# Attention with beacon keys, then a SwiGLU layer, on one core: a new order in the first third of the instruction lists, and the last two projection pairs woven half by half

## The chip, the core and the metric

One core of a Trainium2 chip runs the whole program. The metric is the time of one execution on the device, in microseconds (us), and less is better. A kernel is timed in several executions; the median counts. One more execution is recorded by the hardware profiler, and all rows in this document come from such recordings. Instructions run on five engines, each with its own list in program order: TensorE (PE, with its weight loads shown as PEld), VectorE (DVE), ScalarE (ACT), GpSimd (POOL) and SyncE (SP). They wait for each other through semaphores.

## What is computed

```
scores = scale * np.matmul(q, k_all.transpose(0, 1, 3, 2))   # k_all = [beacon_k, k], 16 + 576 keys
scores = np.where(causal, -1000000000.0, scores)             # beacons are seen by all queries
a = np.exp(scores - scores.max(-1, keepdims=True))
a /= a.sum(-1, keepdims=True) + 1e-09
attn_out = np.matmul(a, v_all)                               # 8 batches, 8 heads, 576 rows, 64 wide
x = attn_out.transpose(0, 2, 1, 3).reshape(B * S, H * D)     # 4608 tokens, 512 wide
g = x @ w_gate                                               # 512 -> 1536
silu = g * (1.0 / (1.0 + np.exp(-g)))
out = (silu * (x @ w_val)) @ w_out                           # 1536 -> 512
```

Inputs and output are float32; the kernel multiplies in bfloat16.

## The kernel before, in words

The 4608 tokens are cut into 9 chunks of 512, the attention into 8 batches of 4 head pairs. All work is cut into small pieces, and one string of letters, `plan` (line 806), says in which order the pieces are written; each letter calls `piece` (line 732), which issues that piece's instructions on whatever engines it needs. So the string sets the order on every engine at once. No scheduler moves anything afterwards. The letters that matter here, each counted from 0 in its own kind:

- `l`: one load on POOL's DMA queue, from the list `order_of_loads` (line 720). From load 24 on (`FREE_LOADS`, line 53) POOL first waits until PE has passed an earlier piece.
- `g`/`f`: pair up q and k of a head pair, on DVE or POOL (the tile `side`). `T`: turn them on PE into a PSUM tile, `t_ps`. `Q`/`q` and `K`/`k`: copy the q half and the k half out of that tile into `qT` and `kT`; the capital letter puts the copy on DVE, the small one on ACT. The two halves lie in two banks of one tile.
- `S`/`s`: the score matmuls of one unit, a quarter of a head pair (`s_ps`). `E`: exp on ACT (`p`). `D`/`M`: the causal mask on DVE or POOL. `P`/`p`: the two halves of the product with v (`pv_ps`). `R`: normalise on DVE (`rec`, then `x`). `X` and `Y`/`y`: turn x of batch 0 on PE, copy it out on DVE or ACT.
- `G`/`H`: the two halves of a gate tile; each is 8 matmuls on 64 of the 128 array rows, which run two at a time (`gv_ps`). `a`: tanh on ACT (`th`). `1`, `2`: two steps on DVE, which write `u` and `hT`.
- `F`: a step of the output projection (`o_ps`), again matmuls on 64 rows in twos. 24 steps make a pair of 128-token tiles. The last of the 18 pairs is cut by columns at 384 into two parts. `O`/`o`: copy a tile out on DVE or ACT and store it.
- `h`: a keep-warm pair, two small matmuls that PE runs ahead of the next score or product piece, into that piece's own PSUM tile (`keep_warm`, line 176).

All PSUM tiles come from four slots of two banks, which `take` and `give` (lines 132 and 140) hand round first in, first out, in the order of the plan. A piece that takes a slot waits until the copy that reads the slot's last tile is done. In `halves` (line 154) the first half of a gate or projection writes one bank with the upper array rows and the other with the lower; the second half swaps them. Before the swap an empty PE instruction waits for the last matmul into the slot:

```
            last = max((w for (i, _), w in writers.items() if i == at[0]), key=lambda w: w[2])
            if was[3]:
                after(nc.tensor.nop(), last[1], "one bank, two row halves")
```

Of the kernel before, what the change touches and what calls it, by code (L numbers as in the profile page):

```python
# [52 lines left out]
FREE_LOADS = 24  # L53
# [33 lines left out]
def kernel(  # L87
# [66 lines left out]
    def halves(key, bank, row, o, l, r, start, stop, turn=False):  # L154
# [3 lines left out]
        if was is not None and was[0] != row:  # L158
            last = max((w for (i, _), w in writers.items() if i == at[0]), key=lambda w: w[2])
            if was[3]:  # L160
                after(nc.tensor.nop(), last[1], "one bank, two row halves")
            for other, w in writers.items():
                if other[0] == at[0]:
                    writers[other] = (w[0], w[1], w[2], False)
# [433 lines left out]
    CUT = 384  # L598

    def project(n):  # L600
        pr, s = divmod(n, 2 * NF)
        j, i = divmod(2 * pr, TOK // P)
        last = pr == NCH * 2 - 1
        parts = [(0, slice(0, DM), s)]
        if last:

            parts = [(0, slice(0, CUT), 2 * s), (0, slice(0, CUT), 2 * s + 1)] if s < NF else [
                (1, slice(CUT, DM), 2 * (s - NF)), (1, slice(CUT, DM), 2 * (s - NF) + 1)]
        for part, cols, st in parts:
            if st == 0:  # L610
                for bank in range(2):
                    key = ("f", pr, part, bank * last)
                    if key not in held:
                        ps = take(key, [P, 2, DM], FP32, "o_ps")
                    projected[pr, part, bank] = key, ps
            second, f = divmod(st, NF)
            for row in (1, 0) if second else (0, 1):
                bank = row ^ second
                key, ps = projected[pr, part, bank]
                k64 = slice(HALF * row, HALF * row + HALF)  # L620
                halves(
                    key, bank, row, ps[:, bank, cols],
                    hTs[j][k64, f, P * (i + bank) : P * (i + bank) + P], wo[k64, f, cols],
                    st == 0, st == 2 * NF - 1,
# [4 lines left out]
    def evacuate(n, eng):  # L629

        pr, bank = divmod(n, 2)
        part, cols = 0, slice(0, DM)
        if pr >= NCH * 2 - 1:
            part, cols = pr - (NCH * 2 - 1), (slice(0, CUT), slice(CUT, DM))[pr - (NCH * 2 - 1)]
            pr = NCH * 2 - 1
# [4 lines left out]
        key, ps = projected[pr, part, bank]  # L640
        copy(eng, o_sb[:, cols], ps[:, bank, cols])
        if bank == 1 or key[-1] != projected[pr, part, 1][0][-1]:
            give(key)
# [88 lines left out]
    def piece(kind):  # L732
        as_kind = {"s": "S", "M": "D", "k": "K", "q": "Q", "Y": "y", "o": "O", "i": "I", "A": "e", "f": "g"}.get(kind, kind)
# [78 lines left out]
    ll2ltGHal1G2lGHHa1aatlt21tGH1H2lattF2aGFH112FF2FFGSaEFlHt1GFFaHa2Gltl1t2GtlH12latH12Fa12FFGGtDHS
    ltlaE1FHFFaG2lSFHtl12allF12GFElMFllFHaSG1FEFHaGFFolMHl2l1G2aSOF1H2FaE1FtFG2sHFEaFslF1FDFlSE2FDFE
    DFSESlPpFFFRlDFFFlStFESSDFFEFFsEDFOPEpMPEOpSFFlFRMStRFEFEFSsFEMEFFDFFPplFSFFFFFlFRDSSEFEtFtSFDFF
    FFFEEFlVFFsoOElFFSFtFFDFtSMPEDEtSFElpSDRFFMFFtlMPtESSFEEpRFttFFGFDDSEGHFGa12HHlla1aG21FHl2aGlFHl
    1a2GSHD1ool2aDtPlEGM1ltp2HRlla1GtlSlGH2alEGHG1l2FaM1HHF2a1GFa2HS1FF2FSFFaEFSFEF12lFSPEFpDMFEFSlS
# [52 lines left out]
```

## Time and profile before

| | |
|---|---|
| median of 3 timed runs | 365.43 us (364.56 to 365.43) |
| span of the profiled execution, first to last instruction | 362.0 us |
| its own time outside the span | not listed; the span is 3.4 us below the median |
| PE busy | 352.9 us, 97% |
| DVE busy | 225.4 us, 62% |
| ACT busy | 187.6 us, 52% |
| POOL busy | 124.6 us, 34% |

A busy share is an average over stages, and a matmul's end in the records is modelled, so that a PE that is 97% busy need not do 97% of what it could. What PE really lost is found from the starts of neighbouring matmuls. In a timeline row, the brackets at the end give the idle time ahead of it and what ended that.

### The profile page before, as it was taken

How to read it: one execution, taken by the hardware profiler on the slowest of the kernel's cores; microseconds unless marked ns; L12 is line 12 of the kernel's file. 1: busy time of each engine (PE TensorE's matmuls, PEld its weight loads, DVE VectorE, ACT ScalarE, POOL GpSimd, SP SyncE). 2: the span in 40 equal slices, each digit the busy share in tenths (PEclk: the TensorE clock that was granted, in tenths of full speed). 3: DMA queues.
4: the chain of work that ended last, by engine and by line, in shares of the span. 5: the costliest groups of instructions: out<-in, count | busy, mean ns of one | idle time of the engine just before them, and what ended most of it. 6: DMA issues, size and time to landing. Idle time of an engine off the chain costs nothing.

```text
span 362.0 us, 11888 instructions
## 1 busy us (share of the span) xinstructions
PE 352.9 (97%) x5160; PEld 198.6 (55%) x5160; DVE 225.4 (62%) x439; ACT 187.6 (52%) x284; POOL 124.6 (34%) x188
## 2 busy tenths in 40 slices
PE   7799999999999999999999999999999999999996
PEld 3587565654444566554565566546655554455544
DVE  5577997566766654487528754776467764464342
ACT  4966999723434777544863576447633232221310
POOL 8945499926247545374423013111000000000000
PEclk9999999999999999999999999999999999999999
DMA  8999999999999999999979829502413000110113
GB/s 121 156 197 204 191 191 158 174 175 147 149 147 121 134 136 129 153 174 135 122 132 147 109 37 154 67 6 26 113 62 65 2 2 0 61 60 1 61 60 116
DMA packets 146132, 39.74 MB, mean 110 GB/s; under 512 B 131488, under 2 KB 141728, under 8 KB 146080
## 3 DMA queue, kind: packets, MB, share of 16 engines
q0 software_dynamic: 97424, 19.00, 72.1%
q1 hardware_dynamic: 48368, 19.79, 27.9%
q8 instruction: 40, 0.66, 0.8%
q10 hardware_dynamic: 288, 0.20, 0.2%
q14 instruction: 12, 0.10, 0.1%
HBM read 38.27 MB, written 9.44 MB: 132 GB/s over the span
## 4 chain that ended last, share of the span: by engine, by line
PE 85%; DMA 5%; POOL 5%; DVE 2%; ACT 1%; issue 1%; POOLq 0%
PE gv_ps L168 49%; PE o_ps L168 25%; DMA qk<-in_q_dram 5%; PE s_ps L168 5%; PE pv_ps L168 4%; PE pv_ps L493 2%; POOL qk L209 2%; POOL vb L219 1%; DVE x L522 1%; POOL wg L248 1%; POOL wv L248 1%; DVE p L414 1%; PE t_ps L166 0%; ACT p L405 0%; ACT th L579 0%
## 5 line engine op out<-in xcount | busy, mean ns | idle before, releaser
L168 PE MATMUL gv_ps<-xT,wv 64*128 64x512 bf16 (+2 forms) x912 | 203.2, 365 | 0.0
L168 PE MATMUL gv_ps<-xT,wg 64*128 64x512 bf16 (+2 forms) x912 | 202.8, 365 | 0.1
L579 ACT ACTIVATE th<-gv_ps 128x512 f32<-128x512 f32 (+2 forms) x114 | 65.4, 575 | 116.5 <-PE gv_ps L168 116.1
L405 ACT ACTIVATE p<-s_ps 128x832 bf16<-128x832 f32 (+2 forms) x127 | 104.3, 868 | 32.4 <-PE s_ps L168 28.7
L168 PE MATMUL o_ps<-wo,hT 64*128 64x512 bf16 (+2 forms) x912 | 116.5, 365 | 0.2
L584 DVE SCALAR_TENSOR_TENSOR u<-th,gv_ps 128x512 f32<-128x512 f32 (+2 forms) x114 | 74.7, 656 | 65.9 <-ACT th L579 65.1
L168 PEld LDWEIGHTS <-wg 64*128 64x128 bf16 x912 | 82.5, 94 | 45.9 <-PE gv_ps L168 2.4
L168 PEld LDWEIGHTS <-wv 64*128 64x128 bf16 x912 | 81.8, 94 | 40.1 <-issue 0.7
L591 DVE SCALAR_TENSOR_TENSOR hT<-gv_ps,u 128x512 bf16<-128x512 f32 (+2 forms) x114 | 74.7, 661 | 3.0
L168 PEld LDWEIGHTS <-hT 64*128 64x128 bf16 x912 | 42.3, 94 | 34.1 <-PE o_ps L168 1.2
L219 POOL DMA_DIRECT2D vb<-in_v_dram x40 | 33.9, 853 | 64.1 <-PE s_ps L168 25.7
L168 PE MATMUL s_ps<-qT,kT 64*128 64x336 bf16 (+3 forms) x512 | 43.0, 250 | 1.9 <-ACT kT L256 1.0
L168 PEld LDWEIGHTS <-kT 64*128 64x128 bf16 x512 | 23.8, 94 | 22.9 <-ACT kT L256 1.8
L219 POOL DMA_DIRECT2D qk<-in_q_dram x25 | 21.2, 851 | 25.7 <-PE gv_ps L168 7.1
L414 DVE TENSOR_TENSOR p<-p,upper 128x256 bf16<-128x256 bf16 (+2 forms) x84 | 24.0, 317 | 9.8 <-ACT p L405 8.1
L522 DVE TENSOR_TENSOR x<-pv_ps,rec 128x640 bf16<-128x640 f32 (+1 forms) x32 | 25.3, 791 | 1.2
L521 DVE RECIPROCAL rec<-pv_ps 128x10 f32<-128x10 f32 (+1 forms) x32 | 6.8, 213 | 28.1 <-PE pv_ps L168 22.7
L258 DVE COPY o_sb<-o_ps 128x512 f32<-128x512 f32 (+2 forms) x20 | 12.7, 654 | 17.0 <-PE o_ps L168 13.9
L219 POOL DMA_DIRECT2D qk<-in_k_dram x25 | 21.3, 856 | 5.4 <-PE gv_ps L168 4.3
L418 POOL TENSOR_SCALAR_AFFINE_SELECT p<-p 128x256 bf16<-128x256 bf16 (+2 forms) x46 | 17.4, 399 | 14.0 <-ACT p L405 13.8
L168 PEld LDWEIGHTS <-p 64*128 64x128 bf16 x960 | 18.8, 94 | 4.5 <-PE pv_ps L168 0.2
L168 PE MATMUL pv_ps<-vb,p 64*128 64x65 bf16 x960 | 19.9, 189 | 0.0
(65 smaller groups left out, 141.4 us busy)
## 6 DMA issues: line engine op xcount, KB each, us to landing
out_dram<-o_sb SPq DMA_DIRECT2D x34, 256.0 KB, 2.6
vb<-in_v_dram POOLq DMA_DIRECT2D x24, 128.0 KB, 5.7
qk<-in_q_dram POOLq DMA_DIRECT2D x21, 128.0 KB, 5.6
qk<-in_k_dram POOLq DMA_DIRECT2D x16, 128.0 KB, 5.9
wo<-in_moe_w_out_dram POOLq DMA_DIRECT2D x2, 768.0 KB, 10.1
wg<-in_moe_w_gate_dram POOLq DMA_DIRECT2D x3, 384.0 KB, 11.7
wv<-in_moe_w_val_dram POOLq DMA_DIRECT2D x3, 384.0 KB, 14.2
qk<-in_k_dram POOLq DMA_DIRECT2D x2, 576.0 KB, 11.5
```

The costliest lines, as they stand in the source:

```text
L168: ins = nc.tensor.matmul(o, lhsT=l, rhs=r, start=start, stop=stop)
L209: return nc.gpsimd.dma_start(qk[b % 2][base : base + HALF, RUN * h0 : RUN * h1] .rearrange("p (h e) -> p h e", e=RUN)[:, :, D * i0 : D * i ...
L219: return nc.gpsimd.dma_start(dst[p0 : p0 + n, c, :, 0:D], src[b, :, r : r + n, :].rearrange("h j d -> j h d"))
L248: nc.gpsimd.dma_start(t[:, :, cols], src[:, cols].rearrange("(kk p) f -> p kk f", p=P))
L258: eng.tensor_copy(o, i)
L405: nc.scalar.activation(p_of(b, m, u == "A")[:, :, c0 : c0 + w], ps[:, :, 0:w], ACT.Exp, scale=0.125)
L414: nc.vector.tensor_tensor(out=ap, in0=ap, in1=upper[:, None, d : d + w].to_broadcast([P, 2, w]), op=ALU.mult)
L418: nc.gpsimd.affine_select(out=ap, in_=ap, compare_op=ALU.is_ge, fill=0.0, base=d, pattern=[[0, 2], [1, w]], channel_multiplier=-1,)
L522: nc.vector.tensor_tensor(out=xs[b][:, c0:NKT, P * m : P * m + P].rearrange("p c (h d) -> p h c d", d=D), in0=o[:, :, :, 0:D], in1=rec[:, ...
L579: nc.scalar.activation(th[:, 0:w], gvs[n][:, 0, 0:w], ACT.Tanh, scale=0.5)
L584: nc.vector.scalar_tensor_tensor(out=u[:, 0:w], in0=ths[n][:, 0:w], scalar=1.0, in1=gvs[n][:, 0, 0:w], op0=ALU.add, op1=ALU.mult)
L591: nc.vector.scalar_tensor_tensor(out=hTs[j][:, f, c0:c1], in0=gvs.pop(n)[:, 1, 0 : c1 - c0], scalar=0.5, in1=ths.pop(n)[:, 0 : c1 - c0], o ...
```

## The change

The order of pieces is new from the first gate half (piece 101 of 1756) to piece 467, some way into the gates of the next chunk but one; the last letters are new too. In the new stretch, five of the eight turns that feed batches 1 and 2 have one copy on DVE and the other on ACT (before: two); the copies of x of batch 0 move from ACT to DVE; four masks move from DVE to POOL; nine keep-warm pairs are added; the loads are marked one by one as free (`L`) or paced (`l`), and those from load 19 to load 58 stand in another order. The last pair is cut at column 320 instead of 384, its parts share one slot per token tile (a bank each), and its steps stand among those of the pair before it. `alone` lets a swap in the last pair wait for its own bank alone.

```diff
-FREE_LOADS = 24
...
-    def halves(key, bank, row, o, l, r, start, stop, turn=False):
+    def halves(key, bank, row, o, l, r, start, stop, turn=False, alone=False):
...
-            last = max((w for (i, _), w in writers.items() if i == at[0]), key=lambda w: w[2])
+            near = [w for w in writers if (w == at if alone else w[0] == at[0])]
+            last = max((writers[w] for w in near), key=lambda w: w[2])
...
-    CUT = 384
+    CUT = 320
+    LAST = NCH * 2 - 1
+    PARTS = (slice(0, CUT), slice(CUT, DM))
+
+    steps = [(pr, 0, f) for pr in range(LAST - 1) for f in range(2 * NF)]
+    for pr, part, half in (
+        (LAST - 1, 0, 0), (LAST, 0, 0), (LAST - 1, 0, 1), (LAST, 1, 0), (LAST, 0, 1), (LAST, 1, 1)
+    ):
+        each = 2 if pr == LAST else 1
+        steps += [(pr, part, f) for f in range(NF * half, NF * half + NF, each)]
...
-                    key = ("f", pr, part, bank * last)
+                    key = ("f", pr, bank * last)
...
+                at = part if last else bank
                 halves(
-                    key, bank, row, ps[:, bank, cols],
+                    key, at, row, ps[:, at, cols],
...
-        if bank == 1 or key[-1] != projected[pr, part, 1][0][-1]:
+        if part if pr == LAST else bank:
             give(key)
...
-        if kind == "l":
-            if n >= FREE_LOADS:
-
+        if kind in "lL":
+            if kind == "l":
                 after(nc.gpsimd.nop(), passed[-2], "paced load")
...
-    PpSyEGXRHElDSylDGaElGH1H2aaXD1lf2Py1pGGlH2GRaXHlylH12aaGGH112a2HG1G2Haa1HaTq2lgGl1H2k1GaS21l2HSE
+    PpSyEGXHRYGhSEaME1LGHaHaDLXM2l1Y2hPp1GGRH2XaYHGlGHHa1212a1Ga12GHa21LLHGG2Hafl1a2TQfHGkl1a2S1EHM2
...
-    FFFOFFFFOFFFOFFFFOFFFFFFFFOo
+    FFFFFOFFFFFFFOFoFFFFFFFFFFFOoFFFFFFOo
```

**First place: the copies out of the turned tiles of batch 1.** ACT's list before the change, at turn 5 (the first head pair of batch 1); both copies stand on ACT, and the first waits for PE alone:

```order
L256 ACTIVATE qT_106<-t_ps 128x576 [waits PE_49]
L256 ACTIVATE kT_108<-t_ps 128x576
L256 ACTIVATE kT_108<-t_ps 128x4x16
L579 ACTIVATE th<-gv_ps 128x272 [waits DVE_49,PE_49]
L405 ACTIVATE p_110<-s_ps 128x2x368 [waits PE_49]
L579 ACTIVATE th<-gv_ps 128x272 [waits DVE_49,PE_49]
```

ACT's list after the change, at the same turn; the q copy is gone to DVE, and the k copy now waits for DVE:

```order
L256 ACTIVATE kT_108<-t_ps 128x576 [waits DVE_49]
L256 ACTIVATE kT_108<-t_ps 128x4x16
L579 ACTIVATE th<-gv_ps 128x272 [waits PE_49,Activation_49]
L405 ACTIVATE p_110<-s_ps 128x2x368 [waits PE_49]
L405 ACTIVATE p_110<-s_ps 128x2x416 [waits PE_49]
```

DVE's list after the change, at turns 6 and 7. Each of the two copies waits for ACT, which copies the other half of its tile first (before the change, turn 6 had both on DVE and turn 7 both on ACT):

```order
L258 COPY qT_106<-t_ps 128x576 [waits Activation_49]
L414 TENSOR_TENSOR p_110<-p_110,upper 128x2x128 [waits Activation_49]
L258 COPY kT_108<-t_ps 128x576 [waits Activation_49]
L584 SCALAR_TENSOR_TENSOR u<-th,gv_ps 128x512
L591 SCALAR_TENSOR_TENSOR hT<-gv_ps,u 128x512 [waits DVE_49]
```

In turns 5 to 7 a copy on one engine now stands behind a copy on another, and gate half 14 takes the slot that turn 7's k copy on DVE gives back.

**Second place: PE's last steps.** Before the change, at the swap inside the last pair's last part (the tile's number tells the token tile); the weight loads wait for PE's own last matmuls:

```order
L168 MATMUL o_ps_7150<-wo_115,hT_6602 128x128
L168 LDWEIGHTS hT_6602 [waits PE_49]
L168 MATMUL o_ps_7149<-wo_115,hT_6602 128x128
L168 LDWEIGHTS hT_6602 [waits PE_49]
L168 MATMUL o_ps_7150<-wo_115,hT_6602 128x128
```

After the change, where the last part's second half begins, behind the last step of the first part:

```order
L168 MATMUL o_ps_7079<-wo_115,hT_6620 128x320
L168 LDWEIGHTS hT_6620 [waits PE_49]
L168 MATMUL o_ps_7078<-wo_115,hT_6620 128x192 [waits DVE_49]
L168 LDWEIGHTS hT_6620 [waits PE_49]
L168 MATMUL o_ps_7079<-wo_115,hT_6620 128x192 [waits Activation_49]
```

The swap stands far behind the first half that it follows; but its matmuls now wait for DVE and ACT, for the copies of the first part out of the same two tiles.

## Rows read from the trace of the kernel before

**Rows 1.** The page: span, engines, and TensorE's clock in 40 slices.
```profile
span 362.0 us, 11888 instructions
...
PE 352.9 (97%) x5160; PEld 198.6 (55%) x5160; DVE 225.4 (62%) x439; ACT 187.6 (52%) x284; POOL 124.6 (34%) x188
...
PEclk9999999999999999999999999999999999999999
```

**Rows 2.** Windows: length, busy PE, PEld, DVE, ACT, POOL (instructions), clock, DMA, GB/s.
```profile
39.00:49.30 10.30, 10.30 (x160) 5.65 (x160) 9.70 (x18) 9.53 (x14) 5.64 (x8) 1.00 1.95 179
49.30:60.00 10.70, 10.42 (x238) 7.59 (x234) 7.67 (x17) 9.56 (x16) 10.70 (x18) 1.00 1.73 183
60.00:72.00 12.00, 11.98 (x208) 7.23 (x204) 8.36 (x19) 9.90 (x13) 11.72 (x17) 1.00 2.34 169
82.00:340.00 258.00, 258.00 (x3512) 138.08 (x3510) 158.54 (x286) 126.09 (x186) 66.06 (x100) 1.00 0.87 92
```

**Rows 3.** The chain that ended last: start, length, what.
```profile
51.07 0.82 DVE x L522
...
53.51 1.69 DVE p L414 x2
...
55.37 0.83 DVE x L522
...
79.46 13.92 PE gv_ps L168 x128
```

**Rows 4.** Timeline of PE around turn 5: start, length, instructions, idle time before.
```profile
32.55 0.44 PE L166 MATMUL t_ps<-ident,side 64*128 64x64 bf16 x18 [0.22 <-POOL side L258]
...
33.28 0.63 PE L168 MATMUL gv_ps<-xT,wg 64*128 64x272 bf16 x2
...
34.56 0.32 PE L168 MATMUL s_ps<-qT,kT 64*128 64x240 bf16 x4
```

**Rows 5.** Timeline of ACT around turns 5 and 7.
```profile
33.13 0.65 ACT L256 ACTIVATE qT<-t_ps 128x576 bf16<-128x576 bf16 x1 [0.37 <-PE t_ps L166]
33.68 0.76 ACT L256 ACTIVATE kT<-t_ps 128x576 bf16<-128x576 bf16 x2
...
38.38 0.60 ACT L579 ACTIVATE th<-gv_ps 128x512 f32<-128x512 f32 x1
39.39 0.78 ACT L405 ACTIVATE p<-s_ps 128x736 bf16<-128x736 f32 x1 [0.42 <-PE s_ps L168]
```

**Rows 6.** Timelines of DVE and ACT at the two turns that already use both.
```profile
61.95 0.75 DVE L258 COPY qT<-t_ps 128x576 bf16<-128x576 bf16 x1
...
62.73 0.65 ACT L256 ACTIVATE kT<-t_ps 128x576 bf16<-128x576 bf16 x1 [0.47 <-DVE qT L258]
...
64.68 0.67 ACT L256 ACTIVATE qT<-t_ps 128x576 bf16<-128x576 bf16 x1
...
65.39 0.76 DVE L258 COPY kT<-t_ps 128x576 bf16<-128x576 bf16 x1 [1.01 <-ACT qT L256]
```

**Rows 7.** Timeline of PE between scores (64 rows) and products with v (128 rows).
```profile
51.22 0.36 PE L493 MATMUL pv_ps<-vb,p 128*128 128x65 bf16 x6 [0.22 <-POOL p L418]
51.51 0.33 PE L168 MATMUL s_ps<-qT,kT 64*128 64x240 bf16 x4
51.77 0.62 PE L493 MATMUL pv_ps<-vb,p 128*128 128x65 bf16 x15
```

**Rows 8.** The end: three pieces of the chain, then DVE's timeline.
```profile
350.01 4.76 PE o_ps L168 x48
...
354.79 2.87 PE o_ps L168 x48
...
357.67 0.89 PE o_ps L168 x24
...
356.94 1.02 DVE L258 COPY o_sb<-o_ps 128x384 f32<-128x384 f32 x2 [2.84 <-PE o_ps L168]
...
358.55 0.29 DVE L258 COPY o_sb<-o_ps 128x128 f32<-128x128 f32 x1 [0.58 <-PE o_ps L168]
```

More of the change, by code (lines that the diff above doesn't have):

```diff
@@ L162, in halves @@
             for other, w in writers.items():
-                if other[0] == at[0]:
+                if other in near:
                     writers[other] = (w[0], w[1], w[2], False)
@@ L597 @@
     projected = {}
-    CUT = 384
+    CUT = 320
[7 more added lines that the diff above has]
+        steps += [(pr, part, f) for f in range(NF * half, NF * half + NF, each)]
     def project(n):
-        pr, s = divmod(n, 2 * NF)
+        pr, part, s = steps[n]
         j, i = divmod(2 * pr, TOK // P)
[L603 to L610, printed above, removed]
+        last = pr == LAST
+        cols = PARTS[part] if last else slice(0, DM)
+        for st in range(s, s + 1 + last):
+            if st == 0 and part == 0:
                 for bank in range(2):
-                    key = ("f", pr, part, bank * last)
+                    key = ("f", pr, bank * last)
                     if key not in held:
                         ps = take(key, [P, 2, DM], FP32, "o_ps")
-                    projected[pr, part, bank] = key, ps
+                    projected[pr, bank] = key, ps
             second, f = divmod(st, NF)
@@ L618, in project @@
                 bank = row ^ second
-                key, ps = projected[pr, part, bank]
+                key, ps = projected[pr, bank]
                 k64 = slice(HALF * row, HALF * row + HALF)
+                at = part if last else bank
                 halves(
-                    key, bank, row, ps[:, bank, cols],
+                    key, at, row, ps[:, at, cols],
                     hTs[j][k64, f, P * (i + bank) : P * (i + bank) + P], wo[k64, f, cols],
-                    st == 0, st == 2 * NF - 1,
+                    st == 0, st == 2 * NF - 1, alone=last,
                 )
@@ L631, in evacuate @@
         pr, bank = divmod(n, 2)
[L632 to L635, printed above, removed]
+        part, cols, at = 0, slice(0, DM), bank
+        if pr >= LAST:
+            part = at = pr - LAST
+            pr, cols = LAST, PARTS[part]
         r = 2 * P * pr + P * bank
@@ L639, in evacuate @@
         o_sb = stored[pr, bank]
-        key, ps = projected[pr, part, bank]
-        copy(eng, o_sb[:, cols], ps[:, bank, cols])
-        if bank == 1 or key[-1] != projected[pr, part, 1][0][-1]:
+        key, ps = projected[pr, bank]
+        copy(eng, o_sb[:, cols], ps[:, at, cols])
+        if part if pr == LAST else bank:
             give(key)
@@ L812 @@
[L812 to L816, printed above, removed]
@@ new lines @@
+    hhhSglELhhhsaEGTHk12lDhSQGTEaSDqKEHGl1ll2SaHSf1DE2a1GEsHS2ElTGEalSHQKlESa1MG2slEM1EMHg2lTaPl1pqk
+    MSsf2PERlsDpElPERSpSFFEEDMRMFlTfFFkQSPFSEEpSFlFFgllFRFSFESSFEFFFEFFlMVlETSFFFFFFDMQEDkTFDFoFSFlO
+    FSFEQKFllSFEFFFEDFDSSPpFFDFDFFFFEFlFEMDDlFRtlsSPpFFlEGEoRSEDPlMHOpRPpGGRGaHt1alHa21Hl2Gltlt1al2G
+    1HHGVa21lll2ltGHal1G2lGHHa1aatlt21tGH1H2lattF2aGFH112FF2FFGSaEFlHt1GFFaHa2Gltl1t2GtlH12latH12Fa1
+    2FFGGtDHSltlaE1FHFFaG2lSFHtl12allF12GFElMFllFHaSG1FEFHaGFFolMHl2l1G2aSOF1H2FaE1FtFG2sHFEaFslF1FD
@@ new lines @@
+    FlSE2FDFEDFSESlPpFFFRlDFFFlStFESSDFFEFFsEDFOPEpMPEOpSFFlFRMStRFEFEFSsFEMEFFDFFPplFSFFFFFlFRDSSEF
+    EtFtSFDFFFFFEEFlVFFsoOElFFSFtFFDFtSMPEDEtSFElpSDRFFMFFtlMPtESSFEEpRFttFFGFDDSEGHFGa12HHlla1aG21F
+    Hl2aGlFHl1a2GSHD1ool2aDtPlEGM1ltp2HRlla1GtlSlGH2alEGHG1l2FaM1HHF2a1GFa2HS1FF2FSFFaEFSFEF12lFSPEF
+    pDMFEFSlSRFFlEFFtSFttEFFDFSFVFFESEtFFFMsMDEFFFDFEsOFSFFolPttDEFDFSpFFEMFsESFRFFFEFFtFPMEGGOtHoSE
+    taplHRPtla11Gpt2HD2tGMRaGSt1HH2tGEa1al2G1HSa2GEH1a2GttHGa12SHH1a2MEG1GaM2DSHHES12FaEFFFFF1FDla2F
@@ L826 @@
+    GFFaHFaFF1FFF12FHa2FG1GFHF2HFaF1FoaFFoFFFFFG2FF1FFHFaF1FGFF2HGFFFaFF12FH2FFaFFFFF1FFFFF2oFFFFFFF
+    FFFFFOFFFFFFFOFoFFFFFFFFFFFOoFFFFFFOo
     """
```

32 lines of the change are left out of this document (13 added, 19 removed).

## The prediction, as made before the run

> **What bounds the kernel now.** I read the page first, then busy time by stage, then the chain of waits, and last the timelines of single engines. The page gives a span of 362.0 us with PE busy for 97% of it, and a granted clock at its upper level, 2.4 GHz, in every slice [rows 1]. How full PE is, the chain tells: 128 gate matmuls of 512 columns take 13.92 us [rows 3]. They run in twos, so a pair takes 0.2175 us, which is 0.425 ns a column, next to nothing over 1/2.4 ns. From 82 to 340 us PE is busy without a break [rows 2], and the starts of its matmuls stand at that spacing nearly throughout. Nothing done ahead of 82 us is therefore made good later: what the early lists lose or gain is carried to the end whole. Adding up column times over 20 to 82 us, I find about 4 us that PE lost there, which is the most that a better order could win. Half are waits, half changes between matmuls on 64 and on 128 rows.
>
> The stage that decides is 39 to 49.3 us. There DVE is busy for 9.70 us of 10.30 and ACT for 9.53 [rows 2]. PE hides nothing for them: every slot that it takes has just been freed. A little later the chain runs through DVE itself (normalising, and a mask pair that holds DVE for 1.69 us) [rows 3]. So in this stretch a delay on DVE or ACT is a delay of PE.
>
> **The early lists, step by step.** I walk both orders with the durations of these rows; a plus is later than before at the same work done.
>
> *Up to turn 5.* Before, PE sits idle for 0.22 us until POOL has paired up the first head pair of batch 1, and a little later gate half H10, straight behind G10, waits for the swap: that row of two matmuls lasts 0.63 us, where single ones last 0.28 [rows 4], some 0.28 us lost. The change does G10 ahead of the turn and the turn between G10 and H10, which hides both: -0.5. Against it stand two keep-warm pairs (2 x 128 columns, 0.11 us), and the three x copies that now queue on DVE ahead of a normalising step, about 0.1. I take **-0.3**.
>
> *Turn 5 to the first score of batch 1.* Before, the turn starts at 32.55, ACT copies q from 33.13 and k from 33.68 for 0.76, and the score starts at 34.56, just when PE has done G10, H10 and G11 behind the turn [rows 4, 5]. Now the k copy waits for q's on DVE. From the turn's start that makes 0.55 until its result is read, 0.75 for q, 0.76 for k, so about 2.1 us. The turn itself takes PE 0.3, and only H10 and G11 are left to cover the rest: 2 x 8 matmuls of 272 columns, four pairs of 0.116 each, 0.93 us. PE waits some 0.85: **+0.85**.
>
> *The next two scores.* Six keep-warm pairs (0.33 us) stand there, ahead of pieces whose slot comes back only with the exp of the delayed score, 0.78 us on ACT [rows 5]. H11 and a score give 0.65 us of other work. Part of the pairs thus fills a wait; I take **+0.3** for pairs and wait together.
>
> *Turn 7 to gate half 14.* Before, both copies were ACT's, and another slot served the next gate. Now G14 takes the slot that the DVE copy of k frees, and that copy waits for q's on ACT, which stands behind an exp (0.78) and a tanh (0.60) [rows 5]: the exp belongs to a score issued just ahead, so q can begin only 0.2 us behind the turn. Then 0.67 + 0.76 us [rows 6]. A score and H13 cover 1.0 us of these 1.8 (8 matmuls of 512 columns are 0.87). PE waits 0.8: **+0.8**.
>
> *The rest of batch 1.* DVE has no slack to catch up [rows 2]: it stood still while ACT copied, and now also pairs up a head pair (before on POOL) that turn 9 waits for. I take **+0.65** by turn 9, and a wait of 0.27 for a late k copy behind it; back come a wait of 0.22 for POOL's mask [rows 7] and part of the stretch in which DVE led the chain [rows 3], -0.5. Together **+0.4**.
>
> *Batch 2.* Products with v now stand singly between scores and projections. In the built list PE changes between 64 and 128 rows 43 times, before 33. What one costs: four score matmuls of 240 and 128 columns start at 51.51, and the product behind them at 51.77 [rows 7]; 368 columns take 0.157, so the change costs 0.10 us. Ten cost 1.0; less 0.2 that the stage above already holds, and less some 0.3 of waits that vanish: **+0.5**. The x transposes of batch 1 start a little later and were due about 0.4 us early; PE too arrives later by as much, so I add nothing.
>
> The other moves I cost at nothing. Loads stand in another order, but by byte count what batch 1 needs lands when it did, and PE comes there later. Four masks on POOL instead of DVE are covered by POOL's slack in that stage (busy 5.64 of 10.30) [rows 2]; if that cover failed, each would cost its wait, 0.2 us as in [rows 7].
>
> Sum of the early lists: -0.3 + 0.85 + 0.3 + 0.8 + 0.4 + 0.5 = **+2.55 us**.
>
> **The end.** The columns stay the same: 512 per step in all. Before, PE waits at three swaps. 48 matmuls from 350.01 are 24 of 512 and 24 of 384 columns, 2.61 + 1.96 = 4.57 us against 4.76; the next 48 are 2.61 against 2.87 [rows 8]; with the reading of the starts, each swap costs 0.22 to 0.25. Weaving puts other work into all three: -0.7. But the last part's second half now waits until DVE and ACT have copied the first part out of the same tiles. That is about 0.16 us from the last matmul to the copy, plus a copy of 320 columns (between 0.29 for 128 and 0.51 for 384 [rows 8], so 0.46), plus 0.05: +0.67. The last copy is 192 columns wide instead of 128 (+0.06), and its store as much larger. Net **0.0**, between -0.7, if the wait were covered, and +0.3.
>
> Against the profiled execution (span 362.0) this makes 364.6. That span is 3.4 us under the median, 365.43, so the forecast is **368.0 us**. A measurement of this kernel tells about 0.3%, 1.1 us, from no change. The bounds: PE's lost time in 20 to 82 us can at most vanish, which with the end gives -3 us or so; on the other side, if the delays of DVE and ACT add up without the gains of 0.3, 0.5 and 0.3 that I put against them, +4 or a little more.
>
> **Rivals.**
>
> *1. Copies of one turn overlap, and the order wins.* If q and k were copied side by side, the waits ahead of the first score and of G14 would fall away (-1.65), DVE would be in step again (-0.9), and if the last wait at the end were covered too, -0.7 more. The sum is 2.55 - 3.25, -0.7 us, and with the waits that I left in place (0.2 at the second score, 0.3 behind turn 9, 0.3 at the x turns) about -1.5: 363.9 us. It decides at turn 5: the k copy must begin with q's. Against it: the two turns that already use both engines show k behind q, 62.73 after 61.95 + 0.75, and 65.39 after 64.68 + 0.67, and both rows name the other copy as what ended their wait [rows 6].
> The Trainium skill, page "PSUM — Partial Sum Buffer", section "PSUM bank collisions raise a hardware error", forbids two engines on one bank only; on other banks they may work at once, and q and k lie in two banks. By that rule the copies could overlap, and the last part could be written while the first is read. Here the program's waits go by tile, and by the rows above the trace does not agree that they overlap. A chance of 0.25, for this and for gains that my walk misses.
>
> *2. Gains and losses balance.* PE may be less tightly bound to DVE than I think, if slots come free earlier. Then only the row changes, the keep-warm pairs (0.5 in all) and one of the two waits of 0.8 stay, 1.0 + 0.5 + 0.8, against the 2 us of waits that were there: +0.3, 365.7. For it: the waits of before are gone for certain. A chance of 0.20.
>
> *3. The delay grows.* DVE masks that meet POOL's pair copies take long (1.69 us for two steps of the chain [rows 3]); if the new order brings more of them together, or the transposes of batch 1 reach chunk 1 late, another 2 us: 370. A chance of 0.07, inside the slower cases.
>
> **How the numbers follow.** The forecast's case has 0.48, rival 3 has 0.07: slower by over 0.3% 0.55. Within 0.3%: rival 2, 0.20. Faster: rival 1, 0.25. The forecast's own range, from sums without the gains and without one wait, is 366.8 to 369.8. To hold 8 in 10, the range reaches over rival 2 and to rival 1 below, 363.8, and up to rival 3: 370.2.
>
> **What would show it.** Right: between the turn near 33 us and the first score of batch 1, PE stands idle for most of a us, and a k copy on ACT starts when q's on DVE ends; a second wait of that size ahead of a gate half near 41 us, ended by a kT copy on DVE; PE some 2.5 us later at 82 us; at the end no swap waits, but one of 0.7 us ended by DVE's or ACT's 320-column copy. Wrong: copies of one turn side by side, or DVE idle between 40 and 50 us, or stretches past 82 us that make up time.

## The result, and the profile after

The changed kernel takes 367.66 us (median of 6 runs, 366.90 to 368.31), the kernel before 365.42 us (6 runs beside it, 364.56 to 365.68). The ratio is 1.0070, with a 95% interval of 1.0052 to 1.0089: slower, by 2.2 us of the 2.6 that the forecast had.

The page of the changed kernel: span, engines and the granted clock in 40 slices.
```profile
span 366.1 us, 11921 instructions
...
PE 355.8 (97%) x5178; PEld 202.3 (55%) x5178; DVE 224.2 (61%) x437; ACT 187.8 (51%) x282; POOL 126.5 (35%) x192
...
PEclk9989999999999999999999999999999999999999
```

The same windows as in [rows 2], and the first 20 us.
```profile
0.00:20.00 20.00, 15.78 (x336) 10.29 (x338) 9.73 (x35) 13.43 (x20) 17.75 (x31) 0.93 1.32 141
39.00:49.30 10.30, 9.46 (x153) 5.49 (x150) 8.15 (x16) 8.54 (x13) 6.47 (x8) 1.00 1.88 164
49.30:60.00 10.70, 10.25 (x215) 6.96 (x212) 9.67 (x18) 9.60 (x15) 9.46 (x17) 1.00 1.63 189
60.00:72.00 12.00, 11.96 (x208) 7.34 (x206) 7.41 (x18) 10.50 (x15) 9.01 (x13) 1.00 1.77 115
82.00:340.00 258.00, 258.00 (x3514) 138.05 (x3510) 160.01 (x288) 125.53 (x185) 69.63 (x104) 1.00 0.95 93
```

PE is as busy as before, 97% of a longer span, so this share says nothing of the loss. The windows say where it is: from 39 to 49.3 us PE now stands idle for 0.84 us, where it had no gap [rows 2], and DVE, busy for 9.70 before, is down to 8.15, since it waits for ACT in between. From 82 us on PE has again no gap: nothing is made good.

The two spans differ by 4.1 us, the medians by 2.2. Part of the 4.1 is not the change's: in the recorded execution the clock was granted at 0.93 in the first 20 us (1.00 before), where both lists are the same. So I count from PE's first x transpose, which stands ahead of all that moved: it starts at 20.33 before and at 21.76 after. Up to the end of PE's last row it is 357.67 + 0.89 - 20.33 = 338.23 us before [rows 8] and 361.56 + 1.17 - 21.76 = 340.97 after: **+2.74 us**.

PE's timeline after: that transpose, turn 5, and each later place where PE waited.
```profile
21.76 0.32 PE L536 MATMUL xt_ps<-ident,x 128*128 128x128 bf16 x3
...
34.36 0.43 PE L166 MATMUL t_ps<-ident,side 64*128 64x64 bf16 x18
...
35.55 0.28 PE L168 MATMUL gv_ps<-xT,wg 64*128 64x272 bf16 x1
36.55 0.33 PE L168 MATMUL s_ps<-qT,kT 64*128 64x240 bf16 x4 [0.72 <-DVE hT L591]
...
37.76 0.34 PE L182 MATMUL s_ps<-ident 64*128 64x128 bf16 x6
...
43.36 0.37 PE L168 MATMUL gv_ps<-xT,wg 64*128 64x512 bf16 x1 [0.63 <-DVE kT L258]
...
46.78 0.35 PE L168 MATMUL s_ps<-qT,kT 64*128 64x336 bf16 x4 [0.21 <-DVE hT L591]
...
54.62 0.35 PE L168 MATMUL s_ps<-qT,kT 64*128 64x336 bf16 x4 [0.17 <-ACT kT L256]
...
57.06 0.35 PE L493 MATMUL pv_ps<-vb,p 128*128 128x65 bf16 x6 [0.29 <-DVE p L414]
...
361.56 1.17 PE L168 MATMUL o_ps<-wo,hT 64*128 64x192 bf16 x24 [0.58 <-DVE o_sb L258]
```

The idle times in brackets run from a modelled end. What PE lost is read from the starts: the last pair of G11 starts at 35.55, a pair takes 0.116 of columns and some issue time, so the score could have started at 35.70, and it came at 36.55: 0.85 us. Read in this way the waits are 0.85, 0.22, 0.74, 0.37, 0.33 and 0.43 us. Between turn 5 and the first score, DVE and then ACT copy:

DVE's timeline after, at turn 5, and at turn 7 behind it.
```profile
34.94 0.76 DVE L258 COPY qT<-t_ps 128x576 bf16<-128x576 bf16 x1
...
42.55 0.76 DVE L258 COPY kT<-t_ps 128x576 bf16<-128x576 bf16 x1 [0.74 <-ACT qT L256]
```

ACT's timeline after, at the same two turns.
```profile
35.73 0.77 ACT L256 ACTIVATE kT<-t_ps 128x576 bf16<-128x576 bf16 x2 [0.77 <-DVE qT L258]
...
41.86 0.66 ACT L256 ACTIVATE qT<-t_ps 128x576 bf16<-128x576 bf16 x1
```

At both turns the second copy starts 0.03 us after the first one ends (34.94 + 0.76 = 35.70, then 35.73; 41.86 + 0.66 = 42.52, then 42.55). The row at 36.55 names a gate step on DVE as what ended PE's wait; that step ends at 36.52, as ACT's k copies do (35.73 + 0.77 = 36.50), and the score needs the k copy, by the program.

### The profile page after: what moved, and what is told of

Same layout as the page of the kernel before. It is cut to its first block, busy times and chain, and to the rows that moved or that the text cites. A ratio compares the mean times of both kernels' runs of the same rounds, so it can differ in the third digit from the quotient of the medians.

```text
span 366.1 us, 11921 instructions
## 1 busy us (share of the span) xinstructions
PE 355.8 (97%) x5178; PEld 202.3 (55%) x5178; DVE 224.2 (61%) x437; ACT 187.8 (51%) x282; POOL 126.5 (35%) x192
## 4 chain that ended last, share of the span: by engine, by line
PE 92%; DVE 3%; ACT 3%; issue 1%
PE gv_ps L168 50%; PE o_ps L168 26%; PE s_ps L168 6%; PE pv_ps L168 4%; PE pv_ps L493 4%; ACT p L405 2%; PE idle_ps L691 1%; PE t_ps L166 1%; DVE hT L591 1%; DVE u L584 1%; DVE p L414 1%; ACT kT L256 1%; DVE qT L258 0%; DVE kT L258 0%; ACT th L579 0%
## 5 line engine op out<-in xcount | busy, mean ns | idle before, releaser
L168 PEld LDWEIGHTS <-hT 64*128 64x128 bf16 x912 | 43.3, 94 | 33.5 <-PE o_ps L168 0.8
L219 POOL DMA_DIRECT2D qk<-in_q_dram x25 | 21.4, 860 | 32.5 <-PE gv_ps L168 18.9
L414 DVE TENSOR_TENSOR p<-p,upper 128x256 bf16<-128x256 bf16 (+2 forms) x80 | 22.2, 310 | 8.1 <-ACT p L405 6.7
L418 POOL TENSOR_SCALAR_AFFINE_SELECT p<-p 128x256 bf16<-128x256 bf16 (+2 forms) x50 | 19.0, 398 | 18.8 <-ACT p L405 18.4
L258 DVE COPY o_sb<-o_ps 128x512 f32<-128x512 f32 (+2 forms) x16 | 10.4, 654 | 18.6 <-PE o_ps L168 15.1
L256 ACT ACTIVATE o_sb<-o_ps 128x512 f32<-128x512 f32 (+2 forms) x22 | 12.7, 580 | 15.3 <-DVE o_sb L258 11.0
```

Of the source, the lines that this page charges most:

```text
L168: ins = nc.tensor.matmul(o, lhsT=l, rhs=r, start=start, stop=stop)
L219: return nc.gpsimd.dma_start(dst[p0 : p0 + n, c, :, 0:D], src[b, :, r : r + n, :].rearrange("h j d -> j h d"))
L256: nc.scalar.activation(o, i, ACT.Copy)
L258: eng.tensor_copy(o, i)
L414: nc.vector.tensor_tensor(out=ap, in0=ap, in1=upper[:, None, d : d + w].to_broadcast([P, 2, w]), op=ALU.mult)
L418: nc.gpsimd.affine_select(out=ap, in_=ap, compare_op=ALU.is_ge, fill=0.0, base=d, pattern=[[0, 2], [1, w]], channel_multiplier=-1,)
```

## Experiments

They carry the numbers of their labels; there is no fourth. Plan edits are given in its letters, with three dots for letters left out. The last column counts as above, from the first x transpose to the end of PE's last row, in one recording of each kernel. Of two kernels with the same early lists it can still differ: experiment 2 has the early lists of before and the same 11.6 us at the end, and stands 0.38 us over before; experiment 3, with the 0.54 us of its shorter end added back, 0.31. So the recording of before was a quick one. The 2.74 is known to some 0.4 us only, and against experiments 2 and 3 it is about 2.4.

The kernel before was run again beside each group of kernels, with medians from 364.76 to 365.42 us. The ratios are to those runs, so kernels are to be compared by ratios and not by medians.

| kernel | median, us | ratio to before, 95% interval | PE, us |
|---|---|---|---|
| before | 365.42 | 1 | 338.23 |
| the change | 367.66 | 1.0070 (1.0052 to 1.0089) | 340.97 |
| e1_old_end | 367.15 | 1.0050 (1.0034 to 1.0067) | 341.30 |
| e2_new_end | 365.41 | 1.0009 (0.9991 to 1.0028) | 338.61 |
| e3_own_tiles | 364.95 | 0.9995 (0.9977 to 1.0013) | 338.00 |
| e5_one_engine | 367.95 | 1.0071 (1.0045 to 1.0097) | 342.51 |
| e6_no_warm | 367.29 | 1.0057 (1.0038 to 1.0075) | 340.53 |
| e7_cover | 367.58 | 1.0062 (1.0040 to 1.0084) | 340.98 |
| e8_no_clash | 367.97 | 1.0074 (1.0047 to 1.0100) | 341.53 |
| e9_best | 364.44 | 0.9977 (0.9958 to 0.9995) | 337.87 |
| e10_rows | 367.42 | 1.0076 (1.0055 to 1.0097) | 341.04 |
| e11_turn5 | 367.46 | 1.0076 (1.0058 to 1.0095) | 340.96 |
| e12_masks | 366.58 | 1.0053 (1.0037 to 1.0069) | 340.09 |
| e13_best2 | 364.43 | 0.9976 (0.9960 to 0.9991) | 337.03 |

**Experiments 1 and 2: each half of the change alone.** Experiment 1 has the new lists and loads with the old end; experiment 2 the old lists and loads with the new end.

Experiment 1 as a diff against the change (`project` and `evacuate` go back as well); experiment 2 is the kernel before with the change's end in the same way.

```diff
-    CUT = 320
+    CUT = 384
...
-    FFFFFOFFFFFFFOFoFFFFFFFFFFFOoFFFFFFOo
+    FFFFFOFFFFFFOFFFFOFFFOFFFFOFFFFFFFFOo
```

> The new early lists and loads with the old end. Theory (the early lists cost about 2.5 us, the end nothing): as slow as the change, 367.4 to 368.0 us, a ratio to the kernel before of about 1.007. Rival A (the early lists are even, the new wait at the end is the loss): back at 365.4 us, a ratio of 1.000.

> The old early lists and loads with the new end. Theory: the three swap waits that go and the one wait that comes balance, 365.4 us, a ratio of 0.999 to 1.001. Rival A: 367.7 us, 1.006. Rival B (weaving is a gain of 0.7 us, and hidden in the change by a larger loss of the early lists): 364.7 us, 0.998.

Measured: experiment 1 is slower than before by 0.34 to 0.67%, experiment 2 the same within 0.3%. PE's time in experiment 1 is 0.33 us over the change's, of which 0.30 is a wait for a weight load that landed late at 26.8 us. In experiment 2 it is 0.38 over before, and none of this lies at the end: up to turn 9 PE is 0.35 us quicker, since POOL's pair copy was ready ahead of turn 5, and behind it come waits of 0.41 us for a load of beacon keys at 50.0 us and of 0.31 for a mask on POOL at 50.7. The last 146 matmuls take 11.6 us with either end. So the end is worth nothing, to within 0.1 us, and the loss is in the early lists. Rivals A and B fall. In experiment 1 the waits stand as in the change, at the same work:
```profile
36.05 0.33 PE L167 MATMUL s_ps<-qT,kT 64*128 64x240 bf16 x4 [0.72 <-DVE hT L590]
...
42.85 0.37 PE L167 MATMUL gv_ps<-xT,wg 64*128 64x512 bf16 x1 [0.63 <-DVE kT L257]
```

**Experiment 3: the new end without its wait.**

```diff
-                    key = ("f", pr, bank * last)
+                    key = ("f", pr, part, bank * last)
...
-        (LAST - 1, 0, 0), (LAST, 0, 0), (LAST - 1, 0, 1), (LAST, 1, 0), (LAST, 0, 1), (LAST, 1, 1)
+        (LAST - 1, 0, 0, 12), (LAST, 0, 0, 12), (LAST - 1, 0, 12, 24), (LAST, 0, 12, 22),
+        (LAST, 1, 0, 12), (LAST, 0, 22, 24), (LAST, 1, 12, 24),
```

> The old early lists with the new end, but each part of the last pair in tiles of its own, and the last part's two halves woven with what is left of the first part. Theory (the wait of 0.64 us ahead of the last 24 matmuls is one for the tile, and all the rest behind it moves up with it): that wait goes and no other comes, 0.5 to 0.6 us less than with the new end as it is: 364.8 us, and in PE's timeline no gap over 0.15 us in the last 20 us. Rival C (the wait only moves, to the slots that the copies of the last pair but one give back, or PE is slowed by copies that run beside it): 365.4 us, and a gap of 0.4 us or more somewhere else among the last 100 matmuls.

PE's end in experiment 2:
```profile
347.91 9.83 PE L168 MATMUL o_ps<-wo,hT 64*128 64x512 bf16 x122
358.32 1.17 PE L168 MATMUL o_ps<-wo,hT 64*128 64x192 bf16 x24 [0.58 <-DVE o_sb L258]
```

And in experiment 3:
```profile
347.76 11.04 PE L168 MATMUL o_ps<-wo,hT 64*128 64x512 bf16 x146
```

There, ACT's copy of the pair before the last, and PE's matmuls behind it in a narrow window:
```profile
355.74 0.60 ACT L256 ACTIVATE o_sb<-o_ps 128x512 f32<-128x512 f32 x1 [6.67 <-DVE o_sb L258]
```
```profile
356.39 0.42 PE L168 MATMUL o_ps<-wo,hT 64*128 64x192 bf16 x6
```

The same 146 matmuls take 358.32 + 1.17 - 347.91 = 11.58 us in experiment 2 and 11.04 here, 0.54 us less. Most of the wait was thus the program's, for the tile. The timeline puts all 146 in one row, but by the starts a wait of 0.20 us is left: PE's matmul at 356.39 follows one at 356.15, and starts 0.05 us after the ACT copy ends (355.74 + 0.60 = 356.34). To this extent rival C is right. The experiment changes two things at once, the tiles and the order of the last steps, and which of them gained how much stays open. The medians agree with the gain (0.46 us) but their intervals overlap.

**Experiment 5: both copies of a turn on one engine.**

```diff
-    ...TQfHGkl1a2...GTHk12lDhSQG...TEaSDqKEHG
+    ...TqfHGkl1a2...GTHK12lDhSQG...TEaSDqkEHG
```

> The change, with both copies of each of turns 5, 6 and 7 on one engine, as before (turn 5 ACT, turn 6 DVE, turn 7 ACT). Theory (the two copies of a turn run one behind the other either way, and only the short cover in PE's list makes the wait): the wait ahead of the first score of batch 1 falls from 0.85 to about 0.6 us, the one ahead of gate half 14 from 0.74 to 0.4 to 0.8 us, the whole is 0.2 to 0.4 us shorter than the change: 367.3 us. Rival D (the split between two engines is what costs): both waits go, about 1.5 us less: 366.2 us.

```profile
35.94 0.33 PE L168 MATMUL s_ps<-qT,kT 64*128 64x240 bf16 x4 [0.47 <-ACT kT L256]
...
40.54 0.37 PE L168 MATMUL gv_ps<-xT,wg 64*128 64x512 bf16 x1 [0.57 <-DVE hT L591]
...
43.12 0.37 PE L168 MATMUL gv_ps<-xT,wg 64*128 64x512 bf16 x1 [0.26 <-ACT kT L256]
```

The first wait fell to 0.60 us and the one ahead of G14 to 0.41, as the theory had it. But a new one of 0.71 us stands ahead of G13: with turn 6's k copy on DVE, the two steps of gate 11 queue behind it, and G13 waits for their slot. In all it is no better than the change: PE's 342.51 us hold a wait of 0.65 for a weight load that landed late at 27.0 us, and 341.86 is still 0.9 more. Up to G14 the new wait and the two shorter ones come to only 0.1 more than in the change; the rest is in two waits behind DVE's masks, near 46.9 us (0.75 for 0.37) and inside the product near 57.5 (0.84 for 0.45). So the split between engines is not what costs (rival D falls), and my sum, with a gain of 0.2 to 0.4, was wrong as well: what ACT and DVE exchange among themselves PE did not get here.

**Experiment 6: without the nine keep-warm pairs.** 
```diff
-    ...RYGhSEaME...Y2hPp1...M2hhhSglELhhhsaE...lDhSQG...
+    ...RYGSEaME...Y2Pp1...M2SglELsaE...lDSQG...
```

> The change without its nine added keep-warm pairs (0.51 us of columns). Theory, as it stands after the last run (from turn 5 to 57 us the copies, exps and masks on ACT and DVE set the pace, and what PE is spared there turns into waits): only the two pairs ahead of turn 5 come off, 0.1 us, and the waits ahead of the scores at 36 to 38 us grow by what the others took: 367.5 us. Rival E (PE sets the pace, as the prediction had it for most of the pairs): 0.4 to 0.5 us less, 367.2 us. Rival F (the pairs keep the clock up): the granted clock falls after a wait between 36 and 45 us, and the time grows by 1 us or more.

PE takes 0.44 us less; the clock stays at its upper level from 28 us on. By PE's time rival E is right and my theory wrong; the intervals of the two ratios overlap. Only one wait grew, by 0.17 us, ahead of the third score, so the three pairs there gave nothing back. The 0.44 is not columns alone: some 0.10 of it is a change between 64 and 128 rows, which went with the pair ahead of a product on 128 rows near 26.4 us. The pairs are written into the score's own tile, so they run behind the wait for that tile's slot and not in it: they delay the score, its exp, and whatever waits for that.

**Experiment 7: filling the wait.**

```diff
-    ...HGkl1a2S1EHM2...
+    ...HGkl1a2HS1EM2...
```

> The change with gate half H11 moved from behind the first score of batch 1 to ahead of it, into the wait of 0.85 us. Theory (ACT and DVE set the pace): the wait at the first score falls to about 0.4 us, the next waits (0.22 ahead of the third score, 0.74 ahead of gate half 14) grow by the same 0.4 us in sum, and the whole stays within 0.2 us of the change, 367.7 us. Rival E (a wait of PE that is filled stays filled): 0.4 us less, 367.2 us.

```profile
36.57 0.33 PE L168 MATMUL s_ps<-qT,kT 64*128 64x240 bf16 x4
...
37.77 0.34 PE L182 MATMUL s_ps<-ident 64*128 64x128 bf16 x6 [0.53 <-ACT p L405]
...
43.37 0.37 PE L168 MATMUL gv_ps<-xT,wg 64*128 64x512 bf16 x1 [0.62 <-DVE kT L258]
```

PE does a gate half in the wait, reaches the first score at the same time (36.57 against 36.55), and waits 0.69 instead of 0.22 us ahead of the third. The third starts at 37.77 against 37.76, G14 at 43.37 against 43.36. Here PE's order decides nothing; the chain from copy to exp to slot does.

**Experiment 8: two masks away from POOL's pair copies.**

```diff
-    ...l2SaHSf1DE2a...pqkMSsf2PERlsDpElP...
+    ...l2SaHSf1ME2a...pqkMSs2PERlfsDpElP...
```

> The change with one mask pair near 45 us moved from DVE to POOL (behind POOL's pair copy instead of beside it), and POOL's pair copy near 55.7 us moved behind one load, so that DVE's mask there does not run beside it. Theory (a DVE mask that runs beside a POOL pair copy takes 0.98 and 1.28 us where it takes 0.47 and 0.28 alone, and DVE sets the pace here): DVE's mask at 55 to 56 us takes 0.3 us, the waits of 0.37 us ahead of the score at 46.8 and of 0.43 us inside the product at 57.1 go or fall below 0.15, the whole is 0.5 to 0.8 us shorter: 367.0 us. Rival G (the masks are no bound, the waits come from elsewhere): both waits stay, 367.7 us.

DVE's timeline, then POOL's, in experiment 8:
```profile
54.64 2.13 DVE L414 TENSOR_TENSOR p<-p,upper 128x256 bf16<-128x256 bf16 x1
```
```profile
54.61 0.85 POOL L219 DMA_DIRECT2D qk<-in_k_dram  x1
55.45 1.16 POOL L258 COPY side<-qk 128x1152 bf16<-128x1152 bf16 x1
```

The wait ahead of the score near 46.8 went. But the mask that I meant to free now met a load that POOL was issuing and then the pair copy, and took 2.13 us where it takes 0.28 alone; PE's wait inside the product grew from 0.43 to 1.28. As a test of the theory's price this run failed. Nor does it show that the load holds the mask. In the kernel before, two masks ran beside the issue of such a load, with no copy behind it, and took their usual time:

DVE's timeline, then POOL's, in the kernel before.
```profile
40.34 0.47 DVE L414 TENSOR_TENSOR p<-p,upper 128x224 bf16<-128x224 bf16 x2
```
```profile
40.19 0.88 POOL L219 DMA_DIRECT2D vb<-in_v_dram  x1 [2.00 <-DMA wv<-in_moe_w_val_dram]
```
In the fourteen recordings 357 of 360 DVE masks that started beside a load alone took 0.22 to 0.29 us; of 19 that started beside a load with a pair copy right behind it, 13 took 0.78 to 2.13. What held this mask for the 0.81 us before the copy's recorded start (54.64, then 55.45) stays open.

**Experiment 10: fewer changes between 64 and 128 rows.**

```diff
-    ...QSPFSEEpSFl...RSEDPlMHOpRPpGGRG...
+    ...QSPpFSEESFl...RSEDPMlOpRPpHGGRG...
```

> The change with two products with v moved up to stand directly behind their first halves (near 60 and 78 us, ahead of a projection step and a score, and ahead of a gate half; a mask of POOL moves ahead of one load with the second). PE then changes four times less between 64 and 128 rows. Theory (each change costs about 0.10 us of PE, and PE sets the pace here): PE ends 0.3 to 0.4 us earlier, counted from its first x transpose at 21.8 us; 367.3 us. Rival H (the changes are hidden, since PE stands ahead of other engines here): within 0.1 us of the change.

Nothing was gained. The gate half that stood between two products had covered a mask on POOL; without it PE waits:
```profile
77.51 0.93 PE L493 MATMUL pv_ps<-vb,p 128*128 128x65 bf16 x25 [0.17 <-POOL p L418]
```
Read from the starts that wait is 0.33 us, and one of 0.15 for an exp stands ahead of it. Counted over the 32.5 us from turn 9 on, the changes fell from 20 to 16 and what PE lost at them from 2.01 to 1.60 us, 0.10 for each; PE's waits in the same stretch rose from 1.15 to 1.67. So the price of a change of rows is as the prediction had it, and what the four saved went into waits.

**Experiment 11: turn 5 earlier.**

```diff
-    ...HGG2Hafl1a2TQfHGkl...
+    ...HGfT2QGHal1a2fHGkl...
```

> The change with turn 5 moved up by two gate halves (ahead of G10 and H9, behind the POOL copy that it needs), and DVE's q copy with it. Theory (the chain turn, q copy, k copy, score, exp sets the pace from turn 5 to gate half 14, so only an earlier turn helps, and all of it): PE waits 0.1 to 0.2 us for POOL ahead of the turn, the wait of 0.85 us ahead of the first score goes, the wait of 0.74 us ahead of gate half 14 stays as it is, and PE ends 0.5 to 0.7 us earlier, counted from its first x transpose: 367.0 us. Rival I (DVE and ACT are busy anyway, and the gain is lost again by gate half 14): the wait there grows by as much, within 0.15 us of the change.

```profile
32.83 0.44 PE L166 MATMUL t_ps<-ident,side 64*128 64x64 bf16 x18
...
35.05 0.27 PE L168 MATMUL gv_ps<-xT,wg 64*128 64x272 bf16 x1 [0.22 <-DVE hT L591]
...
35.51 0.33 PE L168 MATMUL s_ps<-qT,kT 64*128 64x240 bf16 x4
...
42.32 0.37 PE L168 MATMUL gv_ps<-xT,wg 64*128 64x512 bf16 x1 [0.63 <-DVE kT L258]
```

The wait ahead of the first score is gone, yet counted from the first x transpose (20.73) the score starts as late as in the change: 14.78 us against 36.55 - 21.76 = 14.79. DVE's q copy, taken early, held up the steps of gate 8, and gate half 11 waited 0.38 us for their slot; POOL's pair copy cost another 0.19. My chain from the turn was not the whole bound: DVE's list is one too.

**Experiment 12: two masks from DVE to POOL, clear of the pair copies.**

```diff
-    ...l2SaHSf1DE2a...pqkMSsf2PERlsDpElP...
+    ...l2SaHSf1ME2a...pqkMSs2PERsMlfpElP...
```

> The change with two masks moved from DVE to POOL, at 45 and at 55.7 us, both ahead of or clear of POOL's pair copies. Theory (a DVE mask is held until POOL's run of loads and pair copies beside it ends, 2.13 us for one in the eighth run, and DVE's delay is PE's): the waits of 0.37 us ahead of the score at 46.8 and of 0.43 us inside the product at 57.1 go, no wait over 0.5 us comes between 45 and 60 us, and PE ends 0.6 to 0.9 us earlier, counted from its first x transpose: 366.9 us. Rival G (the waits come back elsewhere, as in the eighth run): within 0.15 us of the change.

As expected: the waits of 0.37 and 0.43 us are gone, and PE takes 0.88 us less, more than the two waits together. The time agrees (366.58 us), though its interval still overlaps the change's. By PE's time, of all the edits to the new lists only this one, work taken off DVE, and the one that took work off the score's own path (experiment 6) gained anything.

**Experiments 9 and 13: faster than both kernels.** Both have the old lists and the end of experiment 3; experiment 9 moves POOL's work around two masks (first diff, against experiment 3), experiment 13 moves two masks from DVE to POOL as well (second diff, against experiment 9).

```diff
-    ...ElSEMDlTGMSQaKEHSMM12aGEs1HEa2T1qPpMllkDPfllSpR...
+    ...ElSEMDTGMSQaKEHSMM12aGEs1HEa2T1qPpMflllkDPllSpR...
```

```diff
-    ...ElSEMDTGMSQaKEHSMM12aGEs1HEa2T1qPpMflllkDPllSpRE2sRfsPDpSEE...
+    ...ESEMDTGMSQaKEHSMM12aGEs1HEa2T1qPpMMfllkPSpREMllll2sRfsPpSEE...
```

> The kernel of the third experiment (old early lists, parts of the last pair in tiles of their own) with two moves in POOL's list: one load moved behind the masks of 49 to 52 us, and the pair copy of 53.7 us moved ahead of three loads, away from DVE's masks. Theory: the wait of 0.35 to 0.5 us for POOL's mask inside the product near 51 us goes, DVE's mask pair near 54 us takes 0.47 instead of 1.77 us, so the wait of 0.2 to 0.3 us for the normalising step near 56 us goes as well; with the 0.5 us of the end 1.0 to 1.2 us less than the kernel before: 364.0 us, a ratio of 0.997. Rival G (the waits come back in another place): 0.5 us less than before, as the third experiment, 0.9985.

> The kernel of the ninth run (old early lists, parts of the last pair in tiles of their own) with two more masks moved from DVE to POOL, near 51 and 54.6 us, and two more loads moved behind POOL's masks. Theory (as the last run bore it out: a mask on DVE beside POOL's loads and copies holds DVE, and through the normalising steps PE): no mask on DVE between 46 and 56 us, the waits of the ninth run of 0.41 us for a POOL mask near 50.7 and of 0.46 us for the normalising step near 53.2 fall below 0.15 us each; PE ends 0.5 to 0.8 us earlier than in the ninth run, counted from its first x transpose, and the ratio to the kernel before is 0.995 to 0.997. Rival G (POOL, with the masks behind its pair copy, becomes the next to wait for): a wait of 0.3 us or more for a POOL mask between 52 and 58 us, and no gain over the ninth run, 0.998.

Both are faster than the kernel before, by 0.23 and 0.24%, with intervals that end below 1. In experiment 9 the end is that of experiment 3, with the same wait of 0.20 us left; the rest of the expectation failed, since waits of 0.41 and 0.46 us stayed in other places:
```profile
50.65 1.38 PE L493 MATMUL pv_ps<-vb,p 128*128 128x65 bf16 x40 [0.25 <-POOL p L418]
...
53.16 0.35 PE L168 MATMUL s_ps<-qT,kT 64*128 64x336 bf16 x4 [0.31 <-DVE x L522]
```
In experiment 13 both fell below 0.15 us and one of 0.28 came at 55.2; PE takes 0.84 us less than in experiment 9. About 0.3 of that is chance: PE came 1.4 us later to turn 5 there, and POOL's copy was ready. The medians of the two do not differ, so whether the masks gain beyond the end stays open.

## Why the prediction was right, point by point

The sum of the early lists was 2.55 us, and PE lost 2.74, or about 2.4 against the other recordings with the old lists; the end was to be 0.0, and is. The times of PE's starts, counted from the first x transpose in each trace, show the steps:

| up to the start of | before, us | after, us | difference | predicted so far |
|---|---|---|---|---|
| first score of batch 1 | 34.56 - 20.33 = 14.23 | 36.55 - 21.76 = 14.79 | +0.56 | -0.3 + 0.85 = +0.55 |
| gate half 12 | 35.98 - 20.33 = 15.65 | 38.18 - 21.76 = 16.42 | +0.77 | +0.85 |
| gate half 14 | 40.47 - 20.33 = 20.14 | 43.36 - 21.76 = 21.60 | +1.46 | +1.65 |
| turn 9 | 49.18 - 20.33 = 28.85 | 52.63 - 21.76 = 30.87 | +2.02 | +2.3 |
| end of PE | 338.23 | 340.97 | +2.74 | +2.55 |

*Turn 5 and its score.* The gain of 0.3 ahead of it and the wait of 0.85 came as worked out, the wait to 0.01 us. The k copy starts when q's ends, so rival 1's condition failed in the rows above. What the prediction had not asked is whether the copies alone set this wait: experiments 7 and 11 say that without it PE is no earlier, since DVE's gate steps and ACT's exps behind it are not.

*Next two scores, and G14.* 0.2 and 0.7 us for 0.3 and 0.8. Without the nine pairs 0.44 us come back (experiment 6). That is near the 0.5 that they last, but three of them gave back nothing and 0.10 came from a change of rows, so the agreement is partly luck.

*The rest of batch 1* is the step that failed: "+0.65 by turn 9, and a wait of 0.27" less 0.5 that were to come back. Up to turn 9 it lost 0.56, which is near by luck: 0.37 of it is the wait at 46.78, behind a pair of DVE masks, and PE does not wait ahead of turn 9 for the pair copy that the prediction named. Behind turn 9 the late k copy cost 0.33. The waits of before did go, 1.15 us in all (0.38 for a mask on POOL among them), but new ones of 1.15 came: 0.33 for the k copy, 0.45 inside the product at 57.06, 0.22 for a q copy on DVE, and 0.14. So the 0.5 did not come back. Two masks on DVE had met POOL's pair copies:

DVE's timeline after, then POOL's.
```profile
45.14 0.98 DVE L414 TENSOR_TENSOR p<-p,upper 128x224 bf16<-128x224 bf16 x2
...
55.72 1.28 DVE L414 TENSOR_TENSOR p<-p,upper 128x256 bf16<-128x256 bf16 x1
```
```profile
45.02 0.83 POOL L252 DMA_DIRECT2D wo<-in_moe_w_out_dram  x1
45.84 1.28 POOL L258 COPY side<-qk 128x1152 bf16<-128x1152 bf16 x1
...
55.69 1.16 POOL L258 COPY side<-qk 128x1152 bf16<-128x1152 bf16 x1
```
The mask at 55.72 started behind the copy and was held to its end. Of the pair at 45.14 the first took 0.78 us and the second 0.28; the first stood mostly beside the issue of a load with the copy right behind it, as in experiment 8. That is rival 3's mechanism at the size of two waits, 0.37 and 0.43 us, and experiment 12 took them out.

*Batch 2*, +0.5, had the price right and the balance wrong. Behind turn 9 PE lost 0.7 us where 0.25 was predicted (2.74 - 2.02, against 2.55 - 2.3). From there on it changes between 64 and 128 rows 20 times where it changed 12 times, and loses 2.01 us at the changes for 1.32: this is the 0.7. Waits that went and waits that came balance, where the prediction had 0.5 us less of them over this stretch (0.27, less 0.5, less 0.3). The price stands in PE's timeline after:
```profile
57.35 0.35 PE L168 MATMUL s_ps<-qT,kT 64*128 64x336 bf16 x4
57.63 0.62 PE L493 MATMUL pv_ps<-vb,p 128*128 128x65 bf16 x15
```
The four score matmuls, two of 336 and two of 80 columns in pairs, take 0.17 us at 1/2.4 ns a column, and the product starts 0.28 us behind them: 0.10 for the change. All the changes behind turn 9, read so, take 0.096 to 0.114 us each, but for one of before at 67.08 that waits for a load as well.

*The end.* The three swap waits are gone; the wait for the copies of the first part is 0.7 us by the starts, for 0.67. The zero is a balance of two terms, and experiment 3 took most of the second away (0.54 us).

*From span to time.* The 3.4 us between the recorded span of before and the median proved to be of two kinds: each run of the changed kernel lies 2.0 us above its own span (368.15 and 366.1 in the recorded one), and the runs of before some 1.8, so about 1.6 us are by how much the recorded execution of before was quicker than its median. The medians moved by 2.24 us and PE by 2.74, or 2.4 against experiments 2 and 3; the ratio's interval, 1.9 to 3.3 us, holds all three.

## What to carry to other kernels

Where PE waits on a chain through other engines, as here from copy to exp to slot, reordering PE's list or exchanging work between those engines moved the waits and not the end (experiments 5, 7, 10 and 11). How full those engines were did not tell it: in the changed kernel DVE was busy for 8.15 and ACT for 8.54 of 10.30 us there. What helped was work taken off DVE, or off the path of the piece that the others wait for. Dummy matmuls written into a piece's own tile are on that path. A wait for a tile that another engine still reads can be shortened by giving each part a tile of its own, if enough other work is left to stand between the slot's last reader and its next writer: here 0.54 us of some 0.7 went. And one recording of each kernel told their difference to no better than 0.4 us; a second kernel with the same lists, as experiments 1 and 2 are, shows it.

## What the runs showed of the hardware that I had not expected

A DVE mask of two bf16 operands in SBUF takes 0.28 us alone, and in experiment 8 it took 2.13 us beside POOL's issue of a load and the pair copy behind it; it ended 0.16 us after that copy did (55.45 + 1.16 = 56.61, and 54.64 + 2.13 = 56.77). DVE's gate steps kept their length beside such a copy (0.68 and 0.67 us at 46.05 and 46.65 in the changed kernel, beside the copy from 45.84). The Trainium skill, page "SBUF — State Buffer", section "Who interferes with whom", says that a DVE instruction with two SBUF inputs contends with a GpSimd instruction that reads SBUF; of the DVE modes that use two ports it says that the first to issue has the shared pair for its whole length, and that the other fully blocks. The trace shows the same for the mask at 55.72 us of the changed kernel: POOL's copy had started at 55.69, and the mask ended at 57.00, 0.15 us after the copy (55.69 + 1.16 = 56.85). In experiment 8 the mask's record starts 0.81 us ahead of the copy's, so the order of the records does not tell there which of them is held.

The granted clock differs between executions in code that is the same: it was 0.93 in the first 20 us of the changed kernel's recorded execution and 1.00 in that of before. In the former it stood at its lower level, 1.2 GHz (0.50), from 18 to 20.6 us, although PE had been busy for 1.48 us of the two from 16 to 18 us in both. PE reached its first x transpose anywhere from 20.33 to 22.05 us in the fourteen recordings. So differences of less than 1.5 us between two spans of these recordings say nothing unless both are counted from a common point.
